# A cap on transfers under way, k by position from DRAM, and a new order of the front in a fused attention and MLP kernel

## The chip, the cores and the metric

The kernel runs on one core of one Trainium2 chip. The core has TensorE (PE in the profile, with its weight loads as PEld), VectorE (DVE), ScalarE (ACT), GpSimd (POOL) and SyncE (SP), each with an instruction stream of its own, and 16 DMA engines that move data between DRAM and the on-chip memory SBUF. Matmul results go to PSUM banks. The metric is the device time of one execution in microseconds; lower is better.

## The reference

Three stages follow each other. The first is a linear attention with a decay `lam` per head, in blocks of 64 positions; 2 batches, 8 heads, 768 positions, head size 64:

```python
for b in range(nb):
    sl = slice(b * block, (b + 1) * block)
    qb, kb, vb = (q[:, :, sl], k[:, :, sl], v[:, :, sl])
    intra = np.einsum('bhic,bhjc->bhij', qb, kb) * Dmask[None]
    intra = np.einsum('bhij,bhjd->bhid', intra, vb)
    inter = np.einsum('bhid,bhde->bhie', qb * lam_pow[None], kv_state)
    out[:, :, sl] = intra + inter
    kb_dec = kb * rev_pow[None]
    kv_state = lam_block * kv_state + np.einsum('bhsd,bhse->bhde', kb_dec, vb)
```

Its output, as 1536 tokens of 512 values, is x of an MLP, `max(0.01 * h, h) @ w_out` with `h = x @ w_in` (512 to 2048 to 512). A third stage takes the result through `w_in2` (to 1024), a softmax times its input, a layer norm with a gain, and `w_out2` (back to 512).

## The kernel before, in words

**Attention.** A step `s` (12 of them) is one block of 64 positions for both batches and all heads. The heads stand in 4 pairs; of each pair one head lies in SBUF rows 0 to 63 and the other in rows 64 to 127. `scores_mm(s)` multiplies k and q by channel (32 matmuls of 64x64, one per batch, pair and head), `scores_ev` multiplies by the decay mask on VectorE, which gives `r`. `xs_mm` multiplies v and `r` into the x bank, `state_mm` multiplies k by position and v into the state's bank, `xq_mm` adds the old state times the scaled q (`scale_q`, on GpSimd) to the x bank. `state_ev` adds the state's bank to the decayed old state (`decay_state`, GpSimd). `x_hi` (ScalarE) and `x_lo` (VectorE) split the x bank into a rounded high part and the rest, in `xhi[b]` and `xlo[b]`, where `b` is a block of 512 tokens, four steps.

k is needed twice: by channel for the scores and by position for the state. In DRAM `att` holds, for each block and batch, q by channel, k by channel and k by position side by side. In steps 0 to 2 k by position is not loaded; `turn_mm` makes it from k by channel with 32 matmuls against an identity, and `turn_ev` evicts and scales it on VectorE. From step 3 on `load_turned` loads it, in two transfers of 64 rows each. By channel a head lies in one half of the rows and by position in DRAM in the other, so these loads, and those of v, go to swapped halves (`rows(h)` is `HALF[1 - h]`).

**Weights.** The products are made with high and low parts. Raw weights arrive as 8-byte words in transfers of 512 KB (`load_weights`), and each is converted: `words` (two ScalarE operations), `clamp`, `shift`, `join` (VectorE; `bits` is clamp and shift, `convert` all three), `high` (ScalarE) and `low` (VectorE). A pair `n` of raw tiles is `w_in[n]` (IN) and `w_out[n - 1]` (OUT).

**First MLP.** A unit is 512 tokens by 128 hidden columns: `l1_mm` (12 matmuls of 128x512) into one of two banks, `l1_split` (leaky ReLU and high part `ghi` on ScalarE, low part `glo` on VectorE), `l2_mm` (12 more, into four banks `acc`). There are 48 units. The other eight attention steps are placed between units, `step_at`: after `l1_mm` of units 4, 7, 10, 13 and so on.

**Order.** Every engine runs its instructions in the order of the source: the last lines of the kernel chain each to the one before it on the same engine. So lines 529 to 625, which are the front (four steps of attention and the conversion of the first weights), are an order written out by hand, for all engines at once. All loads but two are issued by SyncE, in the order of the source. A tile pool's buffers come free in turn.

PE's `state_mm` of step 3 stands in unit 3 of the loop (lines 648 to 649), with its addition (672 to 673), which goes through line 225 because no decayed state was made for step 3:

```python
            if i == 3:
                alone(state_mm, NPRE - 1, aps[1])
...
            if i == 3:
                state_ev(NPRE - 1, aps[1])
                decay_state(NPRE, pool)
                scale_q(NPRE, pool)
                scale_k(NPRE, act)
```

Of the kernel before, what the change touches and what calls it, by code (L numbers as in the profile page):

```python
# [23 lines left out]
NS = 12  # L24
DM = 512
# [13 lines left out]


@with_exitstack
def fused_kernel(ctx: ExitStack, tc: tile.TileContext, att, vt, tab, cst, w_in, w_out, w_in2, w_out2, out):

# [27 lines left out]
    dmask = cp.tile([P, NPAIR, CH], F32, name="dmask")  # L71
    qpow = cp.tile([P, NPAIR, CH], F32, name="qpow")
# [31 lines left out]

    def load_step(s):

        t = wp.tile([P, 2048], F32, tag="w", name="ldw")
        qk = t[:, 0:1024].rearrange("p (n c a b) -> p n c a b", n=NB, c=2, a=NPAIR)
        kj, v = (t[:, o : o + 512].rearrange("p (n a b) -> p n a b", n=NB, a=NPAIR) for o in (1024, 1536))
        second = act if s == 0 else sync  # L110
        if s == 0:
            for b, queue in ((0, sync), (1, act)):
                queue.dma_start(out=qk[:, b], in_=att[2 * s + b, :, 0:2])
        else:
# [3 lines left out]
        ld[s] = (qk[:, :, 0], qk[:, :, 1], kj, v)  # L118

    def load_turned(s, kj, v, first, second):  # L120
        for h, queue in ((0, first), (1, second)):
            queue.dma_start(
                out=kj[rows(h)], in_=att[2 * s : 2 * s + 2, HALF[h], 2].rearrange("n p a b -> p n a b")
            )
        if v is None:
            return
        for h, queue in ((0, first), (1, second)):
            queue.dma_start(out=v[rows(h)], in_=vt[s, HALF[h]])
# [4 lines left out]
    def load_qk(s):  # L133
        if s >= NS:
            return
        t = qk_t[s] = ap2.tile([P, NB, 2, NPAIR, CH], F32, tag="qk", name="qk")
        sync.dma_start(out=t, in_=att[2 * s : 2 * s + 2, :, 0:2].rearrange("n p c a b -> p n c a b"))

    def load_kv(s):
        if s >= NS:  # L140
            return
        t = ap1.tile([P, 2, NB, NPAIR, CH], F32, tag="kv", name="kv")
        load_turned(s, t[:, 0], t[:, 1], sync, sync)
        ld[s] = (qk_t[s][:, :, 0], qk_t[s][:, :, 1], t[:, 0], t[:, 1])
# [35 lines left out]
    def scores_mm(s, bank, b, pr):  # L180
        q, k = (qk_t[s][:, :, 0], qk_t[s][:, :, 1]) if s >= NPRE else ld[s][0:2]
        for h in range(2):
            d = rows(h)
            pe.matmul(at(bank, d, b, pr), k[d, b, pr], q[d, b, pr], start=True, stop=True)  # L184

    def scores_ev(s, bank):
        if s >= NS:
            return
        r_t[s] = ap1.tile(SHAPE, F32, tag="r", name="r")
        for src, dst in parts(bank, r_t[s]):  # L190
            mask = dmask if len(src.shape) == 3 else dmask.unsqueeze(1).to_broadcast(SHAPE)
            dve.tensor_tensor(dst, src, mask, op=ALU.mult)

    def turn_mm(s, bank, b, pr):

        for h in range(2):
            d = rows(h)
            pe.matmul(at(bank, d, b, pr), ld[s][K][d, b, pr], delta[d, pr], start=True, stop=True)

    def turn_ev(s, bank, eng):  # L200

        src = bank.rearrange("p (n a b) -> p n a b", n=NB, a=NPAIR)
        if eng is act:
            by_pair(ld[s][KJ], src, dmask)
        else:
            eng.tensor_tensor(ld[s][KJ], src, dmask[:, :, CH - 1 : CH].unsqueeze(1).to_broadcast(SHAPE), op=ALU.mult)

    def state_mm(s, bank, b, pr):

        for h in range(2):  # L210
            j = rows(h)
            pe.matmul(at(bank, j, b, pr), ld[s][KJ][j, b, pr], ld[s][V][j, b, pr], start=True, stop=True)

    def state_ev(s, bank):
        if s >= NS - 1:
            return
        s_t[s + 1] = ap2.tile(SHAPE, F32, tag="s", name="state")
        if s == 0:
            for src, dst in parts(bank, s_t[1]):
                act.copy(dst, src)  # L220
            return
        if s not in sd_t:
            src = bank.rearrange("p (n a b) -> p n a b", n=NB, a=NPAIR)
            for pr in range(NPAIR):
                dve.scalar_tensor_tensor(
                    s_t[s + 1][:, :, pr],
                    s_t[s][:, :, pr],
                    qpow[:, pr, CH - 1 : CH],
                    src[:, :, pr],
                    op0=ALU.mult,  # L230
                    op1=ALU.add,
                )
            return
        for src, dst, old in parts(bank, s_t[s + 1], sd_t[s]):
            dve.tensor_tensor(dst, src, old, op=ALU.add)

    def xs_mm(s, bank, b, pr):

        for h in range(2):
            j = rows(h)  # L240
            pe.matmul(  # L241
                at(bank, HALF[h], b, pr),
                ld[s][V][j, b, pr],
                r_t[s][j, b, pr],
                start=(s == 0 or pr + b == 0),
                stop=(s == 0),
            )

    def xq_mm(s, bank, b, pr):

        for h in range(2):
            d = rows(h)
            pe.matmul(  # L253
# [5 lines left out]
            )  # L259
# [43 lines left out]
    def load_weights(n, halves=None):  # L303
# [9 lines left out]
        if kind == "a":  # L313
            sync.dma_start(out=t.rearrange("p h a b -> p (h a b)"), in_=w_in2[f].bitcast(U32))
            return
        halves = halves or whole(n)
        for i in range(halves.start, halves.stop):
            src = w_out2[f + i] if kind == "b" else w_out[f - 1] if i else w_in[f]
            sync.dma_start(out=t[:, 0 if n == NF else i].rearrange("p a b -> p (a b)"), in_=src.bitcast(U32))
# [184 lines left out]
    def out_mm(t):  # L504
# [5 lines left out]
        for j in range(parts):  # L510
# [7 lines left out]
            sync.dma_start(out=out[t * P : (t + 1) * P, cols], in_=osb[:, cols])  # L518
# [10 lines left out]
    sync.dma_start(out=tabs, in_=tab)  # L529
    load_step(0)  # L530
    load_weights(0)
    load_step(1)
    load_step(2)
    load_weights(1, IN)
    load_step(3)
# [4 lines left out]
    load_turned(NPRE - 1, ld[NPRE - 1][KJ], None, sync, sync)  # L540
# [3 lines left out]
    sync.dma_start(out=fix, in_=cst)  # L544
# [3 lines left out]
    for pr in range(NPAIR):  # L548
        lamj = lams[:, 1, pr : pr + 1].to_broadcast([P, CH])
        dve.tensor_tensor_scan(dmask[:, pr], lamj, delta[:, pr], 0.0, op0=ALU.mult, op1=ALU.add)  # L550
    for pr in range(NPAIR):
        lamd = lams[:, 1, pr : pr + 1].to_broadcast([P, CH])
        dve.tensor_tensor_scan(qpow[:, pr], lamd, zero, 1.0, op0=ALU.mult, op1=ALU.add)

    xb, sb, kt, kb = acc[0:2], acc[2:4], aps[0], aps[1]
    alone(scores_mm, 0, sb[0])
    alone(turn_mm, 0, kt)
    scores_ev(0, sb[0])
    turn_ev(0, kt, dve)
    scale_q(1, pool)  # L560
    both(xs_mm, 0, xb[0], state_mm, 0, kb)
    words(0)
    bits(0)
    state_ev(0, kb)
    x_hi(0, xb[0])
    join(0)
    decay_state(1, pool)
# [36 lines left out]
    x_lo(3, xb[1])
# [4 lines left out]
    convert(1, OUT)  # L609
# [30 lines left out]
    for i, u in enumerate(items[1:], 1):  # L640
# [3 lines left out]
        if i > 1:  # L644
# [137 lines left out]
```

## Time and profile before

| | us |
|---|---|
| median of 3 runs | 469.9 (469.49 to 471.12) |
| the profiled execution, its time | 467.11 |
| its span, first to last instruction | 465.24 |
| PE busy in the span | 448.3 |
| first large product (`l1_mm`, line 418) starts at | 31.80 |
| mean granted TensorE clock | 0.985 |

The profile records one execution. The span is what its rows can explain; about 1.9 us of that execution's time lie around it. The granted clock is given as a share of 2.4 GHz, so 1.00 is 2.4 and 0.50 is 1.2 GHz. Rows of the timeline are: start, duration, engine, line, operation, output and input; in square brackets the time that the engine stood idle before it, and what it waited for ("issue": nothing that the profile shows).

### The profile page before, as it was taken

The page shows a single profiled execution, that of the slowest core. Times are in us where ns is not written, and L with a number is a line of the kernel's source. Part 1 is how long each engine was busy: PE and PEld are TensorE (multiplying, and loading weights), DVE is VectorE, ACT ScalarE, POOL GpSimd, SP SyncE. Part 2 cuts the span into 40 slices and gives each one's busy share as a digit, 9 for nine tenths or more (in the row PEclk, how much of TensorE's full clock was granted, in tenths as well). Part 3 has the DMA queues.
Part 4 walks back from the last instruction along what each step waited for, and adds up shares of the span by engine and source line. Part 5 has one row for each costly group of instructions (what it writes and reads, how often), then busy time and mean ns, then how long its engine had stood idle before and what let it go on. Part 6 is the DMA issues. An engine that isn't in the chain of part 4 may idle for free.

```text
span 465.2 us, 8051 instructions
## 1 busy us (share of the span) xinstructions
PE 448.3 (96%) x3428; PEld 372.0 (80%) x3428; DVE 258.5 (56%) x416; ACT 192.6 (41%) x328; POOL 33.1 (7%) x38
## 2 busy tenths in 40 slices
PE   7589979999999999999999999999999999999996
PEld 5578768888788888888888888888888888888886
DVE  4368888989844121211131789813876666666651
ACT  3148938777643223121244778423222222222221
POOL 1400140210202020100000000000000000000000
PEclk9789989999999999999999999999999999999999
DMA  8998072735303030100025542000000000000001
GB/s 257 353 264 346 2 262 100 271 141 180 92 1 92 1 92 1 48 0 1 0 70 202 182 180 90 1 0 2 0 23 25 23 24 23 24 23 23 24 23 47
DMA packets 16323, 40.83 MB, mean 88 GB/s; under 512 B 1824, under 2 KB 4640, under 8 KB 15776
## 3 DMA queue, kind: packets, MB, share of 16 engines
q1 hardware_dynamic: 16064, 39.93, 24.9%
q8 instruction: 27, 0.44, 0.4%
q10 hardware_dynamic: 224, 0.39, 0.3%
q14 instruction: 8, 0.07, 0.0%
HBM read 37.17 MB, written 3.15 MB: 87 GB/s over the span
## 4 chain that ended last, share of the span: by engine, by line
PE 87%; ACT 4%; DVE 3%; issue 3%; DMA 2%; POOL 1%; SPq 0%; ACTq 0%; POOLq 0%
PE hps L418 25%; PE acc L434 25%; PE acc L514 14%; PE hps L452 7%; PE aps L452 7%; PE acc L492 2%; DMA ldw<-in_att_dram 2%; PE aps L253 1%; PE aps L241 1%; PE acc L184 1%; DVE wio L408 1%; ACT x L333 1%; ACT raww L334 1%; PE acc L253 1%; ACT wio L389 1%
## 5 line engine op out<-in xcount | busy, mean ns | idle before, releaser
L418 PE MATMUL hps<-xhi,wio 128*128 128x512 f32 x384 | 102.9, 390 | 1.5 <-ACT xhi L286 0.9
L425 DVE TENSOR_TENSOR glo<-hps,ghi 128x512 fp32r<-128x512 f32 x48 | 33.2, 692 | 126.6 <-ACT ghi L424 126.2
L434 PE MATMUL acc<-ghi,wio 128*128 128x512 f32 x384 | 97.7, 397 | 0.0
L418 PEld LDWEIGHTS hps<-xhi,wio 128*128 128x128 f32 x384 | 71.8, 188 | 17.4 <-ACT wio L389 1.4
L434 PEld LDWEIGHTS acc<-ghi,wio 128*128 128x128 f32 x384 | 72.4, 191 | 15.5
L421 ACT ACTIVATE hps<-hps 128x512 f32<-128x512 f32 x48 | 28.0, 584 | 125.8 <-PE hps L418 125.8
L418 PE MATMUL hps<-xlo,wio 128*128 128x512 f32 x192 | 51.4, 389 | 0.0
L434 PE MATMUL acc<-glo,wio 128*128 128x512 f32 x192 | 51.3, 389 | 0.0
L514 PE MATMUL acc<-wb,lnhi 128*128 128x512 f32 (+1 forms) x208 | 46.0, 374 | 0.3 <-ACT lnhi L500 0.3
L514 PEld LDWEIGHTS acc<-wb,lnhi 128*128 128x128 f32 x208 | 36.9, 188 | 7.4 <-ACT lnhi L500 0.6
L434 PEld LDWEIGHTS acc<-glo,wio 128*128 128x128 f32 x192 | 36.1, 188 | 7.6
L418 PEld LDWEIGHTS hps<-xlo,wio 128*128 128x128 f32 x192 | 36.0, 188 | 7.6
L333 ACT ACTIVATE x<-raww 128x1024 f32<-128x1024 f32 (+1 forms) x27 | 27.8, 1028 | 12.5 <-DMA raww<-in_w_in_dram 11.0
L350 DVE SCALAR_TENSOR_TENSOR raww<-x,raww 128x1024 uint32<-128x1024 uint32 (+1 forms) x27 | 31.2, 1156 | 0.5
L359 DVE SCALAR_TENSOR_TENSOR x<-x,raww 128x1024 uint32<-128x1024 uint32 (+1 forms) x27 | 30.1, 1114 | 0.8
L424 ACT CAST ghi<-hps 128x512 fp32r<-128x512 f32 x48 | 28.2, 587 | 1.5
L334 ACT ACTIVATE raww<-raww 128x1024 uint32<-128x1024 uint16 (+1 forms) x27 | 27.9, 1033 | 0.0
L484 POOL TENSOR_TENSOR small<-small,nhalf 128x1 f32<-128x1 f32 x12 | 6.6, 550 | 251.3 <-DVE small L483 251.3
L452 PE MATMUL hps<-wa,xhi 128*128 128x512 f32 x96 | 24.2, 394 | 0.0
L452 PE MATMUL aps<-wa,xhi 128*128 128x512 f32 x96 | 24.2, 394 | 0.0
L514 PE MATMUL acc<-wb,lnlo 128*128 128x512 f32 (+1 forms) x104 | 24.0, 373 | 0.0
L472 ACT ACTIVATE e<-hps,small 128x512 f32<-128x512 f32 x12 | 8.2, 686 | 35.9 <-DVE small L470 35.9
(86 smaller groups left out, 534.6 us busy)
## 6 DMA issues: line engine op xcount, KB each, us to landing
raww<-in_w_out_dram SPq DMA_DIRECT2D x23, 512.0 KB, 6.1
raww<-in_w_in_dram SPq DMA_DIRECT2D x16, 512.0 KB, 6.4
qk<-in_att_dram SPq DMA_DIRECT2D x8, 512.0 KB, 4.1
raww<-in_w_in_dram SPq DMA_DIRECT2D x4, 1024.0 KB, 4.8
out_dram<-osb SPq DMA_DIRECT2D x11, 256.0 KB, 2.0
kv<-in_att_dram SPq DMA_DIRECT2D x16, 128.0 KB, 3.4
kv<-in_vt_dram SPq DMA_DIRECT2D x16, 128.0 KB, 3.0
ldw<-in_att_dram SPq DMA_DIRECT2D x3, 512.0 KB, 8.7
```

Of the source, the lines that this page charges most:

```text
L253: pe.matmul(at(bank, HALF[h], b, pr), s_t[s][d, b, pr], qs_t[s][d, b, pr], start=False, stop=(pr + b == NPAIR + NB - 2),)
L333: act.activation(x, raw[:, :, 1].bitcast(F32), AF.Copy, scale=HI_SCALE)
L334: act.activation(raw[:, :, 0], raw.bitcast(U16)[:, :, 1], AF.Copy, scale=LO_SCALE)
L350: dve.scalar_tensor_tensor(raw[:, :, 0], x.bitcast(U32), 3, raw[:, :, 0], op0=ALU.logical_shift_left, op1=ALU.bitwise_or)
L359: dve.scalar_tensor_tensor(xu, xu, 0x80000000, raw[:, :, 0], op0=ALU.bitwise_and, op1=ALU.bitwise_or)
L418: pe.matmul(bank, w[:, s, k], x[b][:, k], start=(i == 0), stop=(i == len(terms) - 1))
L421: act.activation(bank, bank, AF.Prelu, alpha=0.01)
L424: act.copy(ghi, bank)
L425: dve.tensor_tensor(glo, bank, ghi.bitcast(F32), op=ALU.subtract)
L434: pe.matmul(acc[m], w[:, s, m], g, start=(f == 0 and first), stop=(f == NF - 1 and last))
L452: pe.matmul(bank, x[b][:, k, o : o + P], w2_t["a", k, half][:, s], start=(i == 0), stop=(i == len(terms) - 1),)
L514: pe.matmul(po[:, 0:n], x[:, k], w2_t["b", k][:, s, cols], start=(i == 0), stop=(i == len(terms) - 1))
```

## The change

Four things change together.

1. Every transfer goes through a new function `load`, which keeps a list of the transfers in the order of the source and their bytes. A transfer is issued only when the one that lies 1.5 MB (`AHEAD`, 1572864 bytes) back in this list has landed.
2. In steps 0 to 3 q, k by channel and k by position come in one transfer per batch, in rows of 3 KB, and v in one transfer of all 128 rows. Heads by position then lie in their own halves (`jrows`). The turning matmuls and their evictions go; `scale_k` multiplies k by position by the mask's last column instead. A second mask `dfirst` serves these steps; `dmask` is a copy of it with the halves swapped, made by two transfers within SBUF.
3. Since `xs_mm` and `xq_mm` of these steps now read different halves of the rows and add to the same outputs, `xq_mm` waits for an instruction of `state_ev` of the same step.
4. The front's order is written anew; step 3 is finished in the front. The first unit's terms are ordered high, low weights, low x.

The diff, cut to its core:

```diff
+AHEAD = 3 << 19
+    def jrows(s, h):
+        return HALF[h] if s < NPRE else HALF[1 - h]
+    def decay(s):
+        return dfirst if s < NPRE else dmask
+    flight = []
+    def load(queue, out, in_):
+        size = 4
+        for n in out.shape:
+            size *= n
+        ins = queue.dma_start(out=out, in_=in_).ins
+        ahead = size
+        for before, n in reversed(flight):
+            ahead += n
+            if ahead > AHEAD:
+                tc.add_manual_dep(ins, before.name, SYNC, reason="bytes under way")
+                break
+        flight.append((ins, size))
     def load_step(s):
         t = wp.tile([P, 2048], F32, tag="w", name="ldw")
-        qk = t[:, 0:1024].rearrange("p (n c a b) -> p n c a b", n=NB, c=2, a=NPAIR)
...
-            sync.dma_start(out=qk, in_=att[2 * s : 2 * s + 2, :, 0:2].rearrange("n p c a b -> p n c a b"))
-        for h, queue in ((0, sync), (1, second)):
-            queue.dma_start(out=v[rows(h)], in_=vt[s, HALF[h]])
+        qkk = t[:, 0:1536].rearrange("p (n c a b) -> p n c a b", n=NB, c=3, a=NPAIR)
+        v = t[:, 1536:2048].rearrange("p (n a b) -> p n a b", n=NB, a=NPAIR)
+        for b in range(NB):
+            load(act if s + b == 1 and s == 0 else sync, out=qkk[:, b], in_=att[2 * s + b])
+        load(sync, out=v, in_=vt[s])
-    def turn_mm(s, bank, b, pr):
...
+            if s < NPRE and pr + b + h == 0:
+                tc.add_manual_dep(ins, added[s].name, SYNC, reason="another half of rows")
...
-        terms = [(s, k, x) for s, x in ((0, xhi), (0, xlo), (1, xhi)) for k in range(KD)]
+        groups = ((0, xhi), (1, xhi), (0, xlo)) if u == (0, 0) else ((0, xhi), (0, xlo), (1, xhi))
...
-    sync.dma_start(out=tabs, in_=tab)
+    load(sync, out=tabs, in_=tab)
+    scan(dfirst, 0, None)
     load_step(0)
     load_weights(0)
     load_step(1)
+    for h in range(2):
+        load(sync, out=dmask[rows(h)], in_=dfirst[HALF[h]])
     load_step(2)
+    load_step(3)
     load_weights(1, IN)
-    load_step(3)
     load_weights(1, OUT)
     load_weights(2)
     load_weights(3)
     load_qk(NPRE)
-    load_turned(NPRE - 1, ld[NPRE - 1][KJ], None, sync, sync)
     load_kv(NPRE)
```

The front in its new order, after the loads (the old one stands in lines 555 to 625):

```python
    alone(scores_mm, 0, sb[0])
    scale_k(0, dve)
    scores_ev(0, sb[0])
    scan(qpow, 1, 1.0)
    scale_q(1, pool)
    words(0)
    both(xs_mm, 0, xb[0], state_mm, 0, kb)
    state_ev(0, kb)
    x_hi(0, xb[0])
    scale_k(1, act)
    decay_state(1, pool)

    alone(scores_mm, 1, sb[1])
    bits(0)
    scores_ev(1, sb[1])
    x_lo(0, xb[0])
    both(xs_mm, 1, xb[1], state_mm, 1, kb)
    scale_q(2, pool)
    scale_k(2, act)
    alone(scores_mm, 2, sb[0])
    state_ev(1, kb)
    decay_state(2, pool)
    alone(xq_mm, 1, xb[1])
    scores_ev(2, sb[0])
    join(0)
    x_hi(1, xb[1])
    both(xs_mm, 2, xb[0], state_mm, 2, kb)
    x_lo(1, xb[1])
    scale_q(3, pool)
    scale_k(3, act)
    high(0)

    alone(scores_mm, 3, sb[1])
    state_ev(2, kb)
    decay_state(3, pool)
    alone(xq_mm, 2, xb[0])
    scores_ev(3, sb[1])
    both(xs_mm, 3, xb[1], state_mm, 3, kb)
    x_hi(2, xb[0])
    state_ev(3, kb)
    low(0)
    alone(xq_mm, 3, xb[1])
    x_lo(2, xb[0])
    words(1, IN)
    x_hi(3, xb[1])
    bits(1, IN)
    x_lo(3, xb[1])
    words(1, OUT)
    join(1, IN)
    high(1, IN)
    clamp(1, OUT)
    low(1, IN)
    l1_mm((0, 0), hps[0])
    l1_mm((0, 1), hps[1])
    words(2, IN)
    shift(1, OUT)
    join(1, OUT)
```

In the loop's units 2 and 3:

```diff
-            if i == 3:
-                alone(state_mm, NPRE - 1, aps[1])
...
             high(3, OUT)
+            clamp(4)
             low(3, OUT)
-            scale_k(NPRE - 1, act)
-            convert(4)
+            shift(4)
+            join(4)
             words(5)
...
             if i == 3:
-                state_ev(NPRE - 1, aps[1])
+                scale_q(NPRE, pool)
                 decay_state(NPRE, pool)
-                scale_q(NPRE, pool)
                 scale_k(NPRE, act)
```

## Rows read from the trace of the kernel before

**Rows 1.** The head of the page and PE's busy time.

```profile
span 465.2 us, 8051 instructions
...
PE 448.3 (96%) x3428; PEld 372.0 (80%) x3428; DVE 258.5 (56%) x416; ACT 192.6 (41%) x328; POOL 33.1 (7%) x38
```

**Rows 2.** PE's timeline: rows with idle time before them.

```profile
15.80 0.44 PE L184 MATMUL acc<-ldw 64*64 64x64 f32 x8 [1.44 <-issue]
...
22.47 0.79 PE L253 MATMUL acc<-qs,state 64*64 64x64 f32 x9 [3.78 <-issue]
...
31.80 1.20 PE L418 MATMUL hps<-xhi,wio 128*128 128x512 f32 x4 [0.93 <-ACT xhi L286]
...
60.67 0.27 PE L253 MATMUL aps<-qk,state 64*64 64x64 f32 x2 [2.71 <-POOL qk L152]
```

**Rows 3.** PE's waits from 62 us on: total, times, longest.

```profile
PE hps L418 <- ACT wio L389: 0.5, 1, 0.5
```

**Rows 4.** Stretches, busy us and instructions by engine; last PEclk, DMA share, GB/s.

```profile
0.00:8.06 8.06, 6.68 (x96) 3.86 (x100) 2.95 (x10) 1.65 (x3) 0.39 (x6) 1.00 0.80 254
0.00:15.60 15.60, 11.76 (x223) 8.66 (x223) 7.35 (x17) 4.31 (x7) 4.16 (x9) 0.89 0.92 271
15.60:22.00 6.40, 2.89 (x127) 2.75 (x127) 1.89 (x3) 1.25 (x2) 2.28 (x2) 0.90 1.03 366
```

**Rows 5.** Packets by queue: the whole span, then 0.1 us from 13.1.

```profile
q8 instruction: 27, 0.44, 0.4%
...
q8 instruction: 1, 0.02, 72.4%
```

**Rows 6.** Stretches from a block's entry to the next fetch's packet.

```profile
8.06:13.12 5.06, 3.83 (x118) 3.69 (x110) 2.51 (x4) 2.66 (x5) 2.50 (x2) 0.74 1.06 264
...
42.92:43.36 0.44, 0.44 (x15) 0.44 (x16) 0.44 (x1) 0.00 (x0) 0.00 (x0) 1.00 0.98 400
```

**Rows 7.** SP's timeline: the last issue before 8.06 us.

```profile
7.89 0.37 SPq L115 DMA_DIRECT2D ldw<-in_att_dram  x1
```

**Rows 8.** Timelines of PE, ScalarE, VectorE and GpSimd, 48 to 61 us.

```profile
49.67 1.15 PE L212 MATMUL aps<-ldw 64*64 64x64 f32 x32
...
48.37 1.28 ACT L157 ACTIVATE ldw<-ldw,dmask 128x128 f32<-128x128 f32 x4
52.75 1.05 ACT L389 CAST wio<-x 128x1024 fp32r<-128x1024 f32 x1
...
55.23 1.12 DVE L225 SCALAR_TENSOR_TENSOR state<-state,qpow,aps 128x128 f32<-128x128 f32 x4
...
58.36 2.25 POOL L152 TENSOR_TENSOR qk<-qk,qpow 128x512 f32<-128x512 f32 x1
```

**Rows 9.** The chain that ended last: start, us, what.

```profile
61.83 4.49 PE acc L434 x12
66.33 2.74 PE hps L418 x12
```

**Rows 10.** Stretches as in Rows 4: two loads' rates, and the slow group.

```profile
8.00:13.00 5.00, 3.77 (x118) 3.63 (x112) 2.51 (x4) 2.72 (x5) 2.50 (x2) 0.75 1.06 262
...
17.00:24.00 7.00, 3.22 (x104) 3.08 (x95) 1.89 (x3) 1.63 (x3) 2.28 (x2) 0.77 1.02 401
...
61.80:65.10 3.30, 3.30 (x12) 2.62 (x9) 3.18 (x4) 2.69 (x3) 1.37 (x2) 0.50 0.62 204
```

**Rows 11.** Timelines of PE, VectorE and ScalarE: durations of the front's operations.

```profile
4.91 1.15 PE L184 MATMUL acc<-ldw 64*64 64x64 f32 x32
...
6.10 0.69 DVE L192 TENSOR_TENSOR r<-acc,dmask 128x512 f32<-128x512 f32 x1 [0.67 <-PE acc L184]
...
31.16 0.59 ACT L286 CAST xhi<-acc 128x512 fp32r<-128x512 f32 x1
36.03 0.59 ACT L424 CAST ghi<-hps 128x512 fp32r<-128x512 f32 x1
```

**Rows 12.** DMA issues by line: count, KB each, median us to landing.

```profile
out_dram<-osb SPq DMA_DIRECT2D x11, 256.0 KB, 2.0
```

More of the change, by code (lines that the diff above doesn't have):

```diff
@@ L103, in parts, with load_turned @@
         return [(bank.rearrange("p (n a b) -> p n a b", n=NB, a=NPAIR), *operands)]
+    flight = []
[11 more added lines that the diff above has]
+        flight.append((ins, size))
     def load_step(s):
         t = wp.tile([P, 2048], F32, tag="w", name="ldw")
-        qk = t[:, 0:1024].rearrange("p (n c a b) -> p n c a b", n=NB, c=2, a=NPAIR)
[L109 to L114, printed above, removed]
-            sync.dma_start(out=qk, in_=att[2 * s : 2 * s + 2, :, 0:2].rearrange("n p c a b -> p n c a b"))
-        for h, queue in ((0, sync), (1, second)):
-            queue.dma_start(out=v[rows(h)], in_=vt[s, HALF[h]])
[L118 to L128, printed above, removed]
+        qkk = t[:, 0:1536].rearrange("p (n c a b) -> p n c a b", n=NB, c=3, a=NPAIR)
[3 more added lines that the diff above has]
+        load(sync, out=v, in_=vt[s])
+        ld[s] = (qkk[:, :, 0], qkk[:, :, 1], qkk[:, :, 2], v)
+    def load_turned(s, kj, v):
+        for h in range(2):
+            load(sync, out=kj[rows(h)], in_=att[2 * s : 2 * s + 2, HALF[h], 2].rearrange("n p a b -> p n a b"))
+        for h in range(2):
+            load(sync, out=v[rows(h)], in_=vt[s, HALF[h]])
     BOTH = slice(0, 2)
@@ L162, in scale_k @@
             return
-        kj = ld[s][KJ]
+        kj, last = ld[s][KJ], decay(s)
         if eng is act:
-            by_pair(kj, kj, dmask)
+            by_pair(kj, kj, last)
         else:
-            for b in range(NB):
-                eng.tensor_tensor(kj[:, b], kj[:, b], dmask[:, :, CH - 1 : CH].to_broadcast([P, NPAIR, CH]), op=ALU.mult)
+            eng.tensor_tensor(kj, kj, last[:, :, CH - 1 : CH].unsqueeze(1).to_broadcast(SHAPE), op=ALU.mult)
     def decay_state(s, eng):
@@ L183, in scores_mm @@
             d = rows(h)
-            pe.matmul(at(bank, d, b, pr), k[d, b, pr], q[d, b, pr], start=True, stop=True)
+            pe.matmul(at(bank, jrows(s, h), b, pr), k[d, b, pr], q[d, b, pr], start=True, stop=True)
     def scores_ev(s, bank):
@@ L190, in scores_ev @@
         for src, dst in parts(bank, r_t[s]):
-            mask = dmask if len(src.shape) == 3 else dmask.unsqueeze(1).to_broadcast(SHAPE)
+            mask = decay(s) if len(src.shape) == 3 else decay(s).unsqueeze(1).to_broadcast(SHAPE)
             dve.tensor_tensor(dst, src, mask, op=ALU.mult)
-    def turn_mm(s, bank, b, pr):
[L196 to L206, printed above, removed]
     def state_mm(s, bank, b, pr):
         for h in range(2):
-            j = rows(h)
-            pe.matmul(at(bank, j, b, pr), ld[s][KJ][j, b, pr], ld[s][V][j, b, pr], start=True, stop=True)
+            j = jrows(s, h)
+            pe.matmul(at(bank, rows(h), b, pr), ld[s][KJ][j, b, pr], ld[s][V][j, b, pr], start=True, stop=True)
+    added = {}
     def state_ev(s, bank):
@@ L313, in load_weights @@
         if kind == "a":
-            sync.dma_start(out=t.rearrange("p h a b -> p (h a b)"), in_=w_in2[f].bitcast(U32))
+            load(sync, out=t.rearrange("p h a b -> p (h a b)"), in_=w_in2[f].bitcast(U32))
             return
@@ L318, in load_weights @@
             src = w_out2[f + i] if kind == "b" else w_out[f - 1] if i else w_in[f]
-            sync.dma_start(out=t[:, 0 if n == NF else i].rearrange("p a b -> p (a b)"), in_=src.bitcast(U32))
+            load(sync, out=t[:, 0 if n == NF else i].rearrange("p a b -> p (a b)"), in_=src.bitcast(U32))
     def of(n, halves):
@@ L415, in l1_mm @@
         w = win_t[f].rearrange("p s (k c) -> p s k c", k=KD)
-        terms = [(s, k, x) for s, x in ((0, xhi), (0, xlo), (1, xhi)) for k in range(KD)]
+        groups = ((0, xhi), (1, xhi), (0, xlo)) if u == (0, 0) else ((0, xhi), (0, xlo), (1, xhi))
+        terms = [(s, k, x) for s, x in groups for k in range(KD)]
         for i, (s, k, x) in enumerate(terms):
@@ L517, in out_mm @@
             act.copy(osb[:, cols], po[:, 0:n])
[L518 removed]
+            load(sync, out=out[t * P : (t + 1) * P, cols], in_=osb[:, cols])
     c1 = nc.const_aps.tensor(1.0, (P, 1), BF16)
@@ L528, in fused_kernel, with scan @@
     pool.memset(zero, 0.0)
-    sync.dma_start(out=tabs, in_=tab)
+    def scan(table, side, first):
+        for pr in range(NPAIR):
+            lam = lams[:, side, pr : pr + 1].to_broadcast([P, CH])
+            if first is None:
+                dve.tensor_tensor_scan(table[:, pr], lam, delta[:, pr], 0.0, op0=ALU.mult, op1=ALU.add)
+            else:
+                dve.tensor_tensor_scan(table[:, pr], lam, zero, first, op0=ALU.mult, op1=ALU.add)
+    load(sync, out=tabs, in_=tab)
+    scan(dfirst, 0, None)
     load_step(0)
@@ L532, in fused_kernel @@
     load_step(1)
+    for h in range(2):
+        load(sync, out=dmask[rows(h)], in_=dfirst[HALF[h]])
     load_step(2)
+    load_step(3)
     load_weights(1, IN)
-    load_step(3)
     load_weights(1, OUT)
@@ L543, in fused_kernel @@
     load_qk(NPRE + 1)
-    sync.dma_start(out=fix, in_=cst)
+    load(sync, out=fix, in_=cst)
     act.mul(nhalf, one, -0.5)
[L548 to L555, printed above, removed]
+    xb, sb, kb = acc[0:2], acc[2:4], aps[1]
```

81 lines of the change are left out of this document (38 added, 43 removed).

## The prediction

> **What bounds the kernel now.** I read the page's head first: 465.24 us of span, TensorE (PE) busy 96% of it [rows 1]. The rest is little, so next I read PE's idle time in order of time. From the first large product at 31.80 us on, PE stands still for 2.71 us before 60.67 [rows 2], and the waits of the whole stretch after that hold nothing over 0.5 us [rows 3]. So the time is 31.80 us of front, in which the first four attention steps run, plus 433.4 us of nearly dense PE work. Only two things can give much: the front, and that stall.
>
> In the front PE stops before 15.80, 22.47 and 28.32 us for 1.44, 3.78 and 1.09 us, and the view puts all three down to "issue": no operand was late (two of the three stand in [rows 2]). Counting PE's matmuls between these stops shows why: 223 up to the first, then 127, and 127 again [rows 4]. One matmul is a matmul and a weight load, so 127 of them are some 254 instructions. The queue named instruction moves 27 packets, 0.44 MB, so 16 KB each, and 3428 matmuls over 27 packets is 127 each [rows 5]. PE waits for its own program, a block of 127 matmuls at a time, and the block behind the next one is asked for when PE enters a block: at matmul 96 (223 - 127, reached at 8.06 us [rows 4]) for the block from 223 on, at 223 for the one from 350 on, at 350 for the one from 477 on.
>
> The fetch is late because it queues behind data. From entry to the start of its packet 5.06, 4.06, 3.25 and 2.22 us pass in the front, and 0.44 us at 42.92 [rows 6] (five in all, the first and the last shown). In these stretches the queues move 264 x 5.06 = 1.34 MB, then 1.42, 1.07, 0.57 and 400 x 0.44 = 0.18 MB. What was under way at the entry: by 7.89 us 4.07 MB had been issued in the order of the code, and 254 GB/s x 8.06 us = 2.05 MB had moved, so 2.0 MB; by 15.78 us 6.43 MB against 271 x 15.6 = 4.2, so 2.2 MB [rows 4, 7]. The same count by issues gives about 1.3 and 0.6 MB for the next two. So a fetch lets through most of what is under way, up to 1.4 MB. Its own packet takes 72.4% of 16 engines' 0.1 us = 1.16 us [rows 5], and PE resumes 1.5 us after that (13.12 + 1.16 to 15.80). Entry to next block was so 7.74, 6.67 and 5.85 us, while a block of small matmuls is some 3.4 us of PE at full clock (32 + 64 + 31: 1.15 + 1.16 + 1.1, from the rows below) and about 5 at half.
>
> The stall before 60.67 is a chain: the weights' conversions keep VectorE until 55.23, only then comes state 4 (four operations, 1.12 us), then POOL's decay and, behind it, POOL's scaling of q (2.25 us), for which PE waits [rows 8]. The next 12 matmuls take 4.49 us where the other groups take 2.72, at a granted clock of 0.50 [rows 9, 10]: 1.77 us more.
>
> **The change, part by part.** *Order of state 3.* Its 32 matmuls leave the place at 49.67, where they take 1.15 us [rows 8], and go to the front; its addition, and ScalarE's four scalings of k (1.28 us [rows 8]), leave the conversions too. POOL gets q of step 4 scaled before the decay. Both are then done some 20 us before PE wants them, so the stall (2.71) and its slow group (1.77) go: -5.63 us with the 1.15. VectorE and ScalarE lose about a microsecond of work each here, so the conversions keep their place relative to PE, with the margin of about nothing that they have at 53.85 (the high part of pair 4 is ready at 52.75 + 1.05 [rows 8]).
>
> *Turned k from DRAM.* The three groups of 32 turning matmuls go (1.1 us each by the like of them [rows 11]), with their VectorE evictions. The first four steps load 1.05 MB each instead of 0.79 (step 3 earlier got 0.26 MB of k late), and two copies of the mask, 0.13 MB, join the queue. In bytes up to step 3's last load: 4.98 MB after, where 4.36 stood before. In its place each value load of two half-height transfers becomes one of full height. The queue ran at 401 GB/s where large full-height loads were passing and at 262 in a stretch with several halves [rows 10]; I take 385 for the new order. Step 0 lands at about 5.2 us (0.92 MB needed first, 0.66 before: +0.3), step 1 at 9.2, step 2 at 12.5, step 3 at 15.3, the first half of pair 1 at 17.2.
>
> *Matmuls of the front.* 12 + 96 + 3 x 128 = 492 up to the first large product, 556 before. The block limits stay at 96, 223, 350 and 477: now inside the products of step 0, inside scores 2, inside scores 3, and 15 matmuls before the end.
>
> *At most 1.5 MB (1.57 million bytes) under way.* Two prices. It could starve the engines: a transfer with nothing ahead of it, 256 KB, lands 2.0 us after issue [rows 12], of which 0.65 is its bytes, so about 1.35 us is dead time; a load of 0.39 to 0.52 MB needs 2.4 to 2.7 us, and 1.57 MB per 2.7 us is 580 GB/s, above what the engines move. So I price starvation at nothing; the cover is gone if the dead time exceeds some 3 us. It shortens fetches: with 1.57 MB under way the part let through is, between the rows at 2.0 and 1.3 MB, some 1.1 MB, 2.8 us. Entry to next block is then 2.8 + 1.1 + 1.5 = 5.4 us. Bounds: 3.1 us (0.5 + 1.1 + 1.5, the quiet fetch) and 7.7 us (the longest seen). I take 5.4, since 1.57 lies between the two rows.
>
> *New waits.* Each of steps 1 to 3 now lets its second product into x wait for the state's addition on VectorE; behind it stand all later matmuls. Per step: 32 matmuls 1.15 (the next scores' eviction, 0.69, runs beside them), 64 matmuls 1.16 (60.67 to 61.83), addition 0.69 [rows 2, 9, 11]: with the hand-overs 3.4 us at full clock, under one fetch of 5.4. At half clock it is nearer 5.5, about the same. So it hides behind the fetches; where these are quick, it sets the pace.
>
> *Sum of the front.* Scores 0 from 5.2, eviction to 7.1, matmul 96 at 8.1. Block 223 comes at 8.1 + 5.4 = 13.5 (the data would allow 13.1), block 350 at 18.9, block 477 at 24.3. Then 15 matmuls, 0.55, and x's last eviction, 0.59 [rows 11], with hand-overs 1.25: first large product at 25.6 instead of 31.80, -6.2 us. The first term over the low weights instead of the low x keeps it off the last subtraction.
>
> *Behind it.* Joining pair 1's input half and its output words now come after x is complete, one VectorE operation (0.6) and two ScalarE ones (1.2) more than before. Before, the first ghi was ready at 36.03 + 0.59, 0.8 us ahead of its product at 37.39 [rows 11]; now it comes about 1.1 us later relative to the start: +0.4 us.
>
> Total: -6.2 - 5.63 + 0.4 = -11.4 us. Against this execution's own 465.24 us of span (467.11 us of time) that is 453.9 and 455.7; the runs shown have a median of 469.9, 2.8 above the profiled one, and I forecast the median: 458.5.
>
> **The rivals.**
> *Fetches don't shorten* (0.17). If something else than the bytes ahead sets the fetch, it stays at 7.74, 6.67, 5.85: blocks at 15.8, 22.5, 28.4, start at 29.6, only -2.2; total -7.4, 462.5. For it: the waits at 2.0 and 2.2 MB don't rank by bytes. Against it: the wait falls with the queue down to 0.44 us.
> The Trainium skill, "DMA: Bandwidth & Descriptors", section "Queues, rings and completion order", says that an engine takes the queues that have work in turn, a packet at a time; by that a fetch would wait for one packet, the cap would do nothing for it, and the time would be this rival's. By that rule, the trace does not agree: 1.34 MB passed ahead of one fetch.
>
> *Fetches are quick* (0.15). Then steps bind: scores 2 at 12.5, three cycles, start at about 22.0: -9.8 - 5.63 + 0.4, 454.9. For it: 0.44 us at 42.92, though the queue moved 400 GB/s there [rows 6].
>
> *The stall only changes its owner* (0.12). If a conversion or the state of step 4 is late again, 4.5 us stay: -6.9, 463.0. For it: the conversions have no margin, and start 6 us earlier; against it: what went was on the late engines.
>
> *The cap starves the queue: slower* (0.04). At 200 GB/s step 3 lands at 5.3 + (4.98 - 1.18) / 0.2 = 24.3 us and PE starts at some 30; pair 4's raw words, 10.2 MB into the queue, land at 50, where their conversion begins 13 us after the start now, so at 43: -1.8 - 5.63 + 0.4 + 7 = 0. Below that the kernel is slower, at 180 GB/s by some 6 us (476). It decides at a round trip of 7.8 us for 1.57 MB. Against it: the 2.0 us above.
>
> **How the numbers follow.** The forecast's case has 0.52. Its own range is 455.5 to 461: half clock at the first products costs up to 1.8, a fetch longer by 0.8 costs 2.4, one shorter by 0.8 gives 2.4. The range over all cases reaches to the rivals at 454.9 and 463.0, with a little beyond for the medians' own spread: 454 to 464, which leaves out the slow case and edges. 0.3% (1.4 us) is about what can be told from no change: faster 0.94, same 0.02, slower 0.04.
>
> **What would show it.** Stops "issue" of PE in the front, at the same counts of 127, but entry to next block near 5.4 us; first large product near 25.6; no stall over 1 us around step 4, and no half clock there; the queue near 385 GB/s up to 15 us. Wrong would be: blocks still 6 to 8 us apart, gaps in the queue of the first 20 us, PE waiting for VectorE's addition longer than for blocks, or for ghi and converted weights past the start.

## The result, and the profile after

| | before | after |
|---|---|---|
| median, us | 470.51 (4 runs, 469.49 to 472.96) | 457.73 (4 runs, 455.59 to 458.7) |
| profiled execution: time, span | 467.11, 465.24 | 458.31, 456.5 |
| first large product starts at | 31.80 | 24.30 |

The ratio is 0.9715, with a 95% interval of 0.9661 to 0.9768. Forecast were 458.5 (454 to 464) and a span of 453.9. The median agrees to 0.8 us; the profiled span is 2.6 us above its own forecast. So the sum has to be looked at term by term.

The page of after, its head, PE's busy time, and a row of the part on DMA issues (count, KB each, median us from issue to landing):

```profile
span 456.5 us, 7880 instructions
...
PE 441.7 (97%) x3332; PEld 365.0 (80%) x3332; DVE 257.1 (56%) x411; ACT 194.8 (43%) x336; POOL 32.8 (7%) x39
...
ldw<-in_att_dram SPq DMA_DIRECT2D x7, 384.0 KB, 4.9
```

PE lost 96 matmuls and 6.6 us of busy time, some of it by the clock (0.996 on average, 0.985 before), and one of the 27 code fetches went with them. The loads take 4.9 us at the median to land, not the 2.4 to 2.7 that I gave them from the store's 2.0.

After, PE's timeline, the rows with idle time before them that answer to [rows 2]:

```profile
11.07 0.68 PE L196 MATMUL acc<-ldw 64*64 64x64 f32 x16 [0.88 <-DMA ldw<-in_att_dram]
...
14.96 0.68 PE L196 MATMUL acc<-ldw 64*64 64x64 f32 x16 [0.24 <-DMA ldw<-in_att_dram]
...
18.95 0.68 PE L196 MATMUL acc<-ldw 64*64 64x64 f32 x16 [0.89 <-DMA ldw<-in_att_dram]
...
22.47 1.15 PE L254 MATMUL acc<-qs,state 64*64 64x64 f32 x32 [0.88 <-DVE state L236]
24.30 2.11 PE L422 MATMUL hps<-xhi,wio 128*128 128x512 f32 x8 [0.69 <-ACT xhi L289]
...
30.52 2.12 PE L438 MATMUL acc<-ghi,wio 128*128 128x512 f32 x8 [0.48 <-ACT ghi L428]
...
48.01 2.08 PE L422 MATMUL hps<-xhi,wio 128*128 128x512 f32 x4 [2.24 <-ACT wio L392]
```

No stop is put down to "issue" any more, and the 2.71 us before 60.67 are gone. In their place PE waits for data in the front, in step 3 for the state's addition, and before unit 4's first product for a converted weight.

After, the largest of PE's waits up to 24.2 us (total, times, longest):

```profile
PE acc L196 <- DMA ldw<-in_att_dram: 3.9, 6, 1.0
```

After, stretches with the columns of [rows 4]: three from a block's entry to the next fetch's packet, as in [rows 6], then the queue's rate in a long one; below it the same long stretch of the kernel before:

```profile
8.17:10.58 2.41, 1.03 (x41) 0.76 (x32) 1.12 (x2) 1.64 (x4) 0.00 (x0) 1.00 1.06 349
15.07:15.36 0.29, 0.29 (x13) 0.29 (x15) 0.00 (x0) 0.29 (x2) 0.29 (x1) 1.00 0.63 106
19.06:19.84 0.78, 0.78 (x30) 0.78 (x32) 0.18 (x2) 0.78 (x3) 0.78 (x1) 1.00 0.94 373
2.00:24.00 22.00, 15.28 (x490) 12.15 (x488) 12.38 (x24) 9.73 (x24) 6.86 (x6) 1.00 0.92 305
```

```profile
2.00:24.00 22.00, 14.95 (x382) 12.50 (x382) 9.23 (x20) 5.66 (x10) 6.05 (x5) 0.85 1.03 334
```

The fetches wait 2.41, 0.29 and 0.78 us where the first three of before waited 5.06, 4.06 and 3.25, and the queue carries less, 305 GB/s instead of 334. After, the chain that ended last, from 0 to 56 us (start, us, what), is no longer PE's code but loads, one behind the other, up to a conversion:

```profile
8.89 5.10 DMA ldw<-in_att_dram
...
38.81 4.88 DMA raww<-in_w_out_dram
...
43.71 1.17 ACT x L336
...
46.91 1.06 ACT wio L392
...
48.01 4.55 PE hps L422 x12
```

By these rows the difference of the two spans is: start of the first large product 24.30 - 31.80 = -7.50; old stall, its half-clock group and step 3's state matmuls -5.63; first ghi +0.48; the new stall +2.24, and its 12 matmuls at half clock 4.55 - 2.72 = +1.83. Together -8.58; measured -8.74. These are one execution of each kernel; e0 below shows how far another one differs.

### The profile page after: what moved, and what is told of

Read it like the earlier page. It is cut to its first block, busy times and chain, and to the rows that moved or that the text cites. A ratio compares the mean times of both kernels' runs of the same rounds, so it can differ in the third digit from the quotient of the medians.

```text
span 456.5 us, 7880 instructions
## 1 busy us (share of the span) xinstructions
PE 441.7 (97%) x3332; PEld 365.0 (80%) x3332; DVE 257.1 (56%) x411; ACT 194.8 (43%) x336; POOL 32.8 (7%) x39
## 4 chain that ended last, share of the span: by engine, by line
PE 84%; DMA 8%; ACT 3%; DVE 2%; issue 1%; SPq 1%; ACTq 0%
PE hps L422 25%; PE acc L438 25%; PE acc L518 14%; PE hps L456 7%; PE aps L456 7%; DMA ldw<-in_att_dram 3%; PE acc L496 2%; DMA raww<-in_w_out_dram 2%; PE aps L242 1%; DMA raww<-in_w_in_dram 1%; DMA qk<-in_att_dram 1%; PE aps L254 1%; ACT x L336 1%; ACT raww L337 1%; SPq L118 1%
## 5 line engine op out<-in xcount | busy, mean ns | idle before, releaser
L438 PE MATMUL acc<-ghi,wio 128*128 128x512 f32 x384 | 96.2, 393 | 0.5 <-ACT ghi L428 0.5
L438 PEld LDWEIGHTS acc<-ghi,wio 128*128 128x128 f32 x384 | 71.3, 188 | 16.0 <-ACT ghi L428 0.9
L456 PE MATMUL hps<-wa,xhi 128*128 128x512 f32 x96 | 24.2, 394 | 0.0
L456 PE MATMUL aps<-wa,xhi 128*128 128x512 f32 x96 | 24.2, 394 | 0.0
```

What stands on the lines that cost most here:

```text
L438: pe.matmul(acc[m], w[:, s, m], g, start=(f == 0 and first), stop=(f == NF - 1 and last))
L456: pe.matmul(bank, x[b][:, k, o : o + P], w2_t["a", k, half][:, s], start=(i == 0), stop=(i == len(terms) - 1),)
```

## The experiments

The kernels were measured in three groups, each beside the kernel before. Ratios can be compared across groups; medians of different groups only roughly. Medians with their ranges, in us:

| run | what | median | ratio to before (95%) |
|---|---|---|---|
| e0_after_again | the changed kernel again | 458.77 (457.27 to 461.6) | 0.9797 (0.9759 to 0.9834) |
| e1_no_cap | no cap | 459.76 (459.04 to 460.95) | 0.9817 (0.9775 to 0.986) |
| e2_cap_2mb | 2 MB | 456.62 (455.67 to 457.04) | 0.9751 (0.9704 to 0.9798) |
| e3_cap_front | cap for 18 transfers only | 457.46 (455.73 to 461.59) | 0.9778 (0.9714 to 0.9843) |
| e4_before_cap | kernel before, with the cap alone | 463.69 (460.56 to 465.29) | 0.9884 (0.9836 to 0.9932) |
| e5_v_halves | v in two halves | 461.04 (457.99 to 463.86) | 0.9841 (0.9792 to 0.989) |
| e6_2mb_order | 2 MB, two conversions earlier | 458.3 (457.01 to 459.65) | 0.9781 (0.975 to 0.9812) |
| e7_cap_1mb | 1 MB | 469.58 (467.7 to 471.34) | 1.0021 (0.9995 to 1.0048) |
| e8_words5_later | 2 MB, pair 5's words a unit later | 457.87 (456.38 to 460.61) | 0.9785 (0.9749 to 0.9821) |
| e9_2mb_again | 2 MB again | 456.72 (455.24 to 458.34) | 0.9752 (0.9717 to 0.9786) |

The kernel before had medians of 468.6 in the group of e1 to e4, 468.49 in that of e0 and e5 to e7, and 467.56 in that of e8 and e9.

**e1_no_cap.** What does the cap do?

```diff
-AHEAD = 3 << 19
+AHEAD = 1 << 40
```

> The changed kernel with the cap taken off; all else stays. Theory A (the cap shortens PE's code fetches, and thins the data queue): PE stops by issue again at the limits of 127 matmuls, blocks some 6 us apart, first large product at 27 to 28.5 us instead of 24.3, while the queue of the first 24 us moves about 370 GB/s instead of 290 and the stall of 2.24 us before 48 goes with its half clock (4.1 us): about the time of the changed kernel, -1 to +1 us. Rival B (the cap does nothing for fetches; fewer matmuls and full-height loads gave the front): first large product stays at 24.3 or earlier and the stall goes: 4 us faster or more.

PE's timeline, and the stretches from entry to packet, without the cap:

```profile
19.96 0.62 PE L196 MATMUL acc<-ldw 64*64 64x64 f32 x13 [2.79 <-issue]
...
27.69 3.53 PE L422 MATMUL hps<-xhi,wio 128*128 128x512 f32 x8 [0.68 <-ACT xhi L289]
...
50.87 1.20 PE L422 MATMUL hps<-xhi,wio 128*128 128x512 f32 x4 [1.10 <-ACT wio L392]
```

```profile
8.16:11.40 3.24, 1.75 (x62) 1.34 (x52) 1.90 (x4) 3.08 (x8) 1.39 (x2) 1.00 1.04 366
14.03:17.72 3.69, 3.15 (x130) 3.01 (x127) 3.04 (x4) 3.08 (x10) 3.50 (x3) 1.00 1.03 417
19.96:23.78 3.82, 3.81 (x110) 3.82 (x110) 0.69 (x1) 1.39 (x3) 0.00 (x0) 0.57 1.02 411
2.00:24.00 22.00, 15.51 (x458) 12.70 (x456) 10.04 (x20) 9.30 (x23) 7.13 (x6) 0.92 1.02 391
```

The code stops come back, and the fetches let 3.24 x 366 = 1.19 MB, then 1.54 and 1.57 MB pass first; with the cap the three stretches give 0.84, 0.03 and 0.29 MB. So it is the bytes under way that delay a fetch, and the cap removes most of them: the rival "fetches don't shorten" falls. The Trainium skill's rule that the prediction weighed ("DMA: Bandwidth & Descriptors", section "Queues, rings and completion order": queues with work are served in turn) doesn't describe this: 1.57 MB went ahead of one packet. What holds the packet back, no run here shows. Without the cap the queue moves 391 GB/s and the stall before unit 4 is 1.10 us, not 2.24 (it was expected to go): the cap's price is on the same runs. What 1.5 MB are worth beside the new order isn't settled by the times: the ratios of e1 (0.9817) and e0 (0.9797) can't be told apart, and the first measurement gave 0.9715. With 2 MB it is clear: e2, in the same group as e1, is 3.1 us faster, and the ranges don't touch.

**e2_cap_2mb and e9_2mb_again.** The middle.

```diff
-AHEAD = 3 << 19
+AHEAD = 4 << 19
```

> The changed kernel with 2 MB instead of 1.5 MB under way. Theory A: a fetch lets some 0.4 MB more through, about 1 us, and the queue is fuller (330 to 370 GB/s): stops by issue of under 1 us come back, the first large product stays near 24 to 25 us, the stall before 48 shrinks or goes: 2 to 4 us faster than with 1.5 MB. Rival B: 4 us faster or more, and no stop by issue. Rival C (the stall before 48 is the order of conversions, not late data): the stall stays at 2 us.

PE's timeline, and the stretch 2 to 24 us, with 2 MB:

```profile
23.41 0.68 PE L254 MATMUL acc<-qs,state 64*64 64x64 f32 x15 [0.99 <-issue]
24.76 2.11 PE L422 MATMUL hps<-xhi,wio 128*128 128x512 f32 x8 [0.68 <-ACT xhi L289]
...
46.96 1.20 PE L422 MATMUL hps<-xhi,wio 128*128 128x512 f32 x4 [1.10 <-ACT wio L392]
```

```profile
2.00:24.00 22.00, 17.33 (x490) 13.82 (x488) 12.43 (x25) 9.38 (x23) 7.04 (x6) 0.92 1.00 369
```

2 MB costs one code stop of 0.99 us, starts almost as early, and halves the stall; 2 to 4 us less than with 1.5 MB had been expected. Its span is 453.9, by chance the forecast's. Run again it gave the same median:

> 2 MB under way once more, five rounds beside the one above: 455.5 to 457.5 us, the stall before unit 4's products at 1.1 us. If it only was a lucky set before: 458 us or more, as with 1.5 MB.

456.6 and 456.7 against 457.7 and 458.8 for 1.5 MB are the lowest medians seen, by some 1.6 us. But the two caps were not timed in one group, and by the ratios, 0.9751 and 0.9752 against 0.9715 and 0.9797, neither is shown to be the faster one.

**e7_cap_1mb.** Can the cap starve the queue?

```diff
-AHEAD = 3 << 19
+AHEAD = 2 << 19
```

> The changed kernel with 1 MB under way. Theory A (bytes under way over the round trip of some 5 us set the rate): the queue moves 200 to 230 GB/s in the first 24 us, no code stops, step 3 lands near 22 us, first large product at 27 to 29, pair 5's words at 50 or later with a stall of 4 us or more: 464 to 470 us. Rival (a round trip of 2.7 us per load as I priced it): the queue still moves 350 GB/s or more and the time is that of the changed kernel or less, with shorter fetches.

PE's timeline, and the stretch, with 1 MB:

```profile
13.59 1.12 PE L196 MATMUL acc<-ldw 64*64 64x64 f32 x16 [3.16 <-DMA ldw<-in_att_dram]
...
60.73 2.07 PE L422 MATMUL hps<-xhi,wio 128*128 128x512 f32 x4 [7.47 <-ACT wio L392]
```

```profile
2.00:24.00 22.00, 15.78 (x405) 12.39 (x407) 9.72 (x20) 7.63 (x20) 6.15 (x6) 0.84 0.75 234
```

Yes: at 234 GB/s PE never waits for code, but it waits 3.16 us for data and 7.47 us for weights (and 2.74 us for the first ghi), and the whole gain is gone. That is what the slower rival describes, one step of the cap away. With the other runs, the last column being the median of the 384 KB loads from issue to landing in that stretch:

| cap | GB/s, 2 to 24 us | cap divided by rate, us | loads landed after, us |
|---|---|---|---|
| 1 MB | 234 | 4.5 | 3.6 |
| 1.5 MB | 305 | 5.2 | 5.0 |
| 2 MB | 369 | 5.7 | 5.4 |
| none | 391 | | 6.5 |

The rows of that column for 1 MB, 2 MB and no cap:

```profile
ldw<-in_att_dram SPq DMA_DIRECT2D x6, 384.0 KB, 3.6
```

```profile
ldw<-in_att_dram SPq DMA_DIRECT2D x6, 384.0 KB, 5.4
```

```profile
ldw<-in_att_dram SPq DMA_DIRECT2D x6, 384.0 KB, 6.5
```

With 1 MB the quotient is longer than the landing, so on average less than the cap was under way.

**e4_before_cap.** The cap alone, on the kernel before: `queue.dma_start(` becomes `load(queue, ` for every transfer, nothing else moves.

> The kernel before with the cap of 1.5 MB on all its transfers, nothing else. Theory A: stops by issue shrink or go, first large product at 27 to 29.5 instead of 31.8 us; the stall before 60.7 (state 3) stays: 2 to 5 us faster than before. Rival B: no change of the stops; the thinner queue makes it equal or slower.

PE's timeline, the kernel before with the cap:

```profile
15.50 0.45 PE L203 MATMUL acc<-ldw 64*64 64x64 f32 x8 [1.08 <-issue]
...
19.97 0.50 PE L272 MATMUL acc<-qs,state 64*64 64x64 f32 x9 [1.58 <-issue]
...
25.34 0.96 PE L272 MATMUL acc<-qs,state 64*64 64x64 f32 x14 [2.65 <-issue]
...
30.11 1.20 PE L437 MATMUL hps<-xhi,wio 128*128 128x512 f32 x4 [0.68 <-ACT xhi L305]
...
58.94 0.27 PE L272 MATMUL aps<-qk,state 64*64 64x64 f32 x2 [2.70 <-POOL qk L171]
```

The stops shrink only from 6.31 to 5.31 us in all, the start comes 1.7 us earlier, but later than the 27 to 29.5 expected, and the stall of 2.70 stays. So the stall's removal belongs to the rest of the change. By the medians the cap alone gives some 5 us (463.69 against 468.6); the profiled executions differ by 1.8 us only (this one was the slowest of its seven), so the trace accounts for no more than that. Parts 2 to 4 of the change without the cap (e1) give some 9, all together 9.7 to 12.8. Parts 2 to 4 were not run apart.

**e5_v_halves.** Is a value load of full height worth anything?

```diff
-        load(sync, out=v, in_=vt[s])
+        for h in range(2):
+            load(sync, out=v[HALF[h]], in_=vt[s, HALF[h]])
```

> The changed kernel with v of steps 0 to 3 loaded as two transfers of 64 rows, each into its own half, instead of one of 128. Theory A (a transfer to half of the rows moves at about half the rate): each step's data come 0.6 us later, and the cap lets a landing delay the next issue, so the first large product moves from 24.3 to 26 to 27 us: 1 to 3 us slower than the changed kernel. Rival (height does not matter, only bytes): within 0.7 us of it.

PE's timeline and the stretch, with halves:

```profile
27.69 2.14 PE L423 MATMUL hps<-xhi,wio 128*128 128x512 f32 x8 [0.69 <-ACT xhi L290]
```

```profile
2.00:24.00 22.00, 15.05 (x409) 12.50 (x410) 9.30 (x20) 7.68 (x20) 7.22 (x6) 0.84 0.92 281
```

The same bytes in halves move at 281 instead of 308 GB/s (e0, same group), the first large product starts at 27.69 instead of 25.97, and the median is 2.3 us higher, with ranges that overlap. Two executions of the unchanged kernel differ by as much in that start (24.30 and 25.97), and halves are also twice as many transfers of v, so whether the height costs anything stays open.

**e3_cap_front.** If the cap is dropped behind the front, does the stall go?

```diff
+CAPPED = 18
...
-            if ahead > AHEAD:
+            if ahead > AHEAD and len(flight) < CAPPED:
```

> The changed kernel with the cap on the first 18 transfers only (up to the words of pair 1). Theory A: the front stays as it is (24.3 us, no stop by issue over 0.5 us up to block 477), the later loads fill the queue, pair 5's words land before 40 us instead of 43.7, and the stall of 2.24 us and its half clock go: 4 us faster than the changed kernel. Rival B: the same gain, but not more than without any cap. Rival C (order of conversions): the stall before 48 stays.

PE's timeline with the cap for 18 transfers only:

```profile
27.13 1.11 PE L255 MATMUL acc<-qs,state 64*64 64x64 f32 x15 [1.77 <-issue]
...
52.87 1.20 PE L423 MATMUL hps<-xhi,wio 128*128 128x512 f32 x4 [1.06 <-ACT wio L393]
```

Only half of it was right. The stall falls to 1.06 us, so the other 1.2 us were the late words of pair 5, which stand ahead of the conversion on ScalarE (the DMA at 38.81 in the chain above). But a code stop of 1.77 us before 27.13 returns: the queue fills before the last fetch of the front, which lets some 1.0 MB pass in 3.4 us. The median, 457.46, can't be told from those of 1.5 MB (457.73 and 458.77); the execution shown was the slowest of its four.

**e6_2mb_order and e8_words5_later.** What holds the last 1.1 us? The first makes pair 1's join and words before the last `x_hi` and `x_lo`, the second takes pair 5's words and clamp off the way (both with 2 MB):

```diff
     alone(xq_mm, 3, xb[1])
     x_lo(2, xb[0])
     words(1, IN)
-    x_hi(3, xb[1])
     bits(1, IN)
-    x_lo(3, xb[1])
-    words(1, OUT)
     join(1, IN)
+    words(1, OUT)
+    x_hi(3, xb[1])
+    x_lo(3, xb[1])
```

> 2 MB under way, and the join of pair 1's input half on VectorE as well as the output half's words on ScalarE before the last step's split of x. Rival C for the rest of the stall (1.10 us of it stays at 2 MB and without a cap): VectorE's conversions, saturated from the first product on, set it; they then begin 0.6 to 1 us earlier, the stall falls to 0.1 to 0.5 us, 0.5 to 1 us faster than 2 MB alone (456.6). If late data set the rest: the stall stays at 1.1 us.

The stall was 1.08 us: missed. Doing that join earlier on VectorE doesn't bear on it.

```diff
             join(4)
-            words(5)
...
-            clamp(pair_at(i, 2))
+            if i > 3:
+                clamp(pair_at(i, 2))
...
             low(pair_at(i, 1))
             if i == 3:
                 scale_q(NPRE, pool)
                 decay_state(NPRE, pool)
                 scale_k(NPRE, act)
+                words(5)
+                clamp(5)
```

> 2 MB under way, and the words of pair 5 on ScalarE (2.2 us) moved behind the high part of pair 4 and the scaling of k of step 4, with pair 5's clamp behind pair 4's low part. If ScalarE's order sets the rest of the stall (its chain of waits runs through these words): the stall of 1.10 us before unit 4's products falls under 0.3 us, 1 us faster than 2 MB alone. If VectorE's join of pair 4 sets it (it ends 0.03 us before ScalarE is free): the stall stays at 1.0 to 1.1 us, same time.

The stall stays at 1.06 us. ScalarE is free now and waits itself; its timeline and VectorE's, with pair 5's words later:

```profile
46.33 1.04 ACT L392 CAST wio<-x 128x1024 fp32r<-128x1024 f32 x1 [1.50 <-DVE x L362]
```

```profile
45.07 1.23 DVE L362 SCALAR_TENSOR_TENSOR x<-x,raww 128x1024 uint32<-128x1024 uint32 x1
```

So VectorE's join of pair 4 (line 362) is enough to set this half of the stall: without ScalarE's words it is the same. From the eviction of step 4's scores to that join VectorE works all but without a gap (0.69 us idle in the kernel before, none with 2 MB). First rows of the kernel before, PE then VectorE, then of 2 MB, with GpSimd's row last:

```profile
42.92 1.15 PE L184 MATMUL hps<-qk 64*64 64x64 f32 x32
...
53.85 1.20 PE L418 MATMUL hps<-xhi,wio 128*128 128x512 f32 x4
```

```profile
44.12 0.69 DVE L192 TENSOR_TENSOR r<-hps,dmask 128x512 f32<-128x512 f32 x1 [0.76 <-PE hps L184]
44.73 0.68 DVE L408 TENSOR_TENSOR wio<-x,wio 128x512 fp32r<-128x512 f32 x1
...
51.08 1.23 DVE L359 SCALAR_TENSOR_TENSOR x<-x,raww 128x1024 uint32<-128x1024 uint32 x1
```

```profile
36.29 1.15 PE L196 MATMUL hps<-qk 64*64 64x64 f32 x32
```

```profile
37.49 0.69 DVE L204 TENSOR_TENSOR r<-hps,dmask 128x512 f32<-128x512 f32 x1 [0.19 <-PE hps L196]
38.10 1.28 DVE L411 TENSOR_TENSOR wio<-x,wio 128x512 fp32r<-128x512 f32 x1
...
44.60 1.23 DVE L362 SCALAR_TENSOR_TENSOR x<-x,raww 128x1024 uint32<-128x1024 uint32 x1
```

```profile
37.53 1.30 POOL L165 TENSOR_TENSOR qk<-qk,qpow 128x512 f32<-128x512 f32 x1 [17.73 <-PE hps L196]
```

VectorE needs 52.31 - 44.12 = 8.19 us before and 45.83 - 37.49 = 8.34 us with the change. PE came to unit 4's product 53.85 - 42.92 = 10.93 us after the scores; now it is ready for it after 46.96 - 1.10 - 36.29 = 9.57. PE gained 1.36 us there, while the conversion itself begins only 0.26 us earlier after the scores' eviction (45.86 - 37.49 = 8.37 against 52.75 - 44.12 = 8.63): the difference is the stall of 1.10.

VectorE's chain would have been shorter, since its 0.69 us of idle time are gone, but two of the same operations take longer there while GpSimd scales q and decays the state of step 4, which the new order put beside them: the low part of a weight half takes 1.28 us instead of 0.68, and the next clamp 0.68 instead of 0.42, together 0.86 us. The changed kernel, e0, e1, e2 and e8 all show the two. No run moved GpSimd's work or shortened VectorE's chain by itself, so what that would give back isn't shown.

**e0_after_again.** The changed kernel beside its variants:

> The changed kernel once more, beside the next three on the same chip: 455.5 to 459 us; the first large product at 24 to 25 us, a stall of 1.1 to 2.5 us before unit 4's products.

A span of 456.2, the first large product at 25.97 with one code stop of 0.43 us, and the stall again, 2.32 us, here with its products at full clock (1.00). The start was expected at 24 to 25; in this execution step 1's data came later (its scores began at 10.33 us, not at 9.51). So the stall belongs to the kernel, while its 1.83 us of half clock belong to some executions.

## Why the prediction was right, and where it was wrong

**Right: the fetches.** PE's stops were its code waiting behind data, and fewer bytes ahead shorten the wait: e1 against the changed kernel shows it. The limits did stay where the counts of 127 put them. The value of 5.4 us from entry to next block was mis-sized: blocks came as early as PE could use them, 6.90, 3.99 and some 3.9 us apart. I had taken the bytes let through as 1.1 of the 1.57 MB that may be under way; measured were 0.84, 0.03 and 0.29 MB. Only the first fetch, 2.41 us, comes near: 5.1 us by the same sum. In e0 the third one lets some 0.7 MB pass and leaves the stop of 0.43 us, so the value varies from one execution to the next.

**Mis-sized, the other way: data.** I had step 1's loads land at 9.2 us, step 2's at 12.5 and step 3's at 15.3. PE took up the last halves of their scores at 11.07, 14.96 and 18.95, each time after waiting for data. The step that failed is "a load of 0.39 to 0.52 MB needs 2.4 to 2.7 us ... so I price starvation at nothing". Its dead time came from a store with nothing ahead of it; loads with up to 1.57 MB under way need 4.9 us, and the queue moved 305 GB/s (1.57 MB per 5.2 us), not 385. The two errors cancel in the front: -7.50 for the forecast -6.2, or, with e0's 25.97, -5.8. The slower rival's mechanism is real, though it decides earlier than I worked out: with 1 MB the kernel is level with the one before at 234 GB/s already, not at 200.

**Wrong: the stall goes.** The old one did go, with its half clock, as the order of state 3 said; e4 keeps both the old order and the stall. But "the stall only changes its owner", given 0.12, came true beside the forecast's case: 4.07 us in the profiled execution. The failing step is "VectorE and ScalarE lose about a microsecond of work each here, so the conversions keep their place relative to PE". VectorE's lost addition stood behind the conversions (55.23 [rows 8], against a join that ended at 52.31), and two operations ahead of the join grew by 0.86 us beside GpSimd, which the sum had at nothing; so the chain to pair 4's join kept its 8.2 us, while PE lost its 1.15 us of state 3 ahead of the product, where the margin was nothing. ScalarE's lost 1.28 us did stand ahead of the conversion, but brought it only 0.26 us, since the join then decides. That makes 1.1 us of the stall; the other 1.1 us are late words, the cap again (e2 and e3 take them away).

**Mis-sized, small.** The wait of `xq_mm` for the state's addition was to hide behind fetches; with these gone it shows once, 0.88 us in step 3. Taking it away wasn't tried, since the wait orders additions to the same outputs. The late ghi was +0.48 for +0.4 in the profiled execution; e0 and e2 show no such wait. The lower end of the forecast's own range was a slip: its terms reach down to 456.1, not 455.5.

**The total.** The forecast was a gain of 11.4 us. The profiled executions differ by 8.8 us of time, the medians by 12.8 in the first measurement and 9.7 in e0's group. The kernel before had been profiled in one of its quicker executions (467.11 in runs from 465.88 to 472.96), and I forecast the median by adding that offset; the changed kernel was profiled in an execution slower than its median (458.31 against 457.73). So that 458.5 met the median to 0.8 us was partly luck: a better front, a new stall, and two offsets of opposite sign. It isn't proof of each term.

## What to carry to other kernels

Where a kernel starts with megabytes of loads queued, look for PE stops named "issue" at a constant number of matmuls: its code may be waiting behind the data, and a cap on bytes under way frees it. The cap must be measured at several sizes: the rate that it leaves goes by how long a load takes in a loaded queue (some 5 us here), not in an idle one (2.0). When work leaves an engine, mark on each chain whether it stood ahead of the late operation or behind it: PE lost 1.15 us ahead of the product, VectorE its share behind the join, and the difference came back as a stall. Look also at what now runs side by side: VectorE's operations grew where GpSimd's were moved to. A total that agrees is worth a second look at its terms.

## What the runs showed of the hardware that was not expected

- A load's time to landing grows with what may be under way: a 384 KB load took 3.6 us with 1 MB, 5.0 with 1.5, 5.4 with 2 MB and 6.5 without a cap (medians of six), against 2.0 us for a 256 KB store late in the kernel.
- With the same 256 KB in two transfers of 64 rows the whole queue moved 281 instead of 308 GB/s over 22 us, in one execution of each.
- The same VectorE operation took 1.28 us while GpSimd scaled q, and 0.68 us without.
- After a PE stop of 2.24 us the granted clock was 0.50 in one execution (4.55 us for the 12 products) and after one of 2.32 us it was 1.00 in another; what decides between them stays open.
